# One attention and routing kernel: a unit's x and the last blocks of q and k are transposed at another place

## The chip, the core and the metric

The kernel runs on one core of one Trainium2 chip. The metric is the device time of one launch in microseconds (us). Before the change the median of three runs is 667.53 us (664.54 to 668.78).

## The reference

Two blocks follow each other. The first is attention over a sliding window of 64 keys, for 8 batches, 8 heads, 576 positions and heads of width 64:

```
scores = scale * np.matmul(q, k.transpose(0, 1, 3, 2))
mask = (rel >= 0) & (rel < window)
scores = np.where(mask, scores, -1000000000.0)
attn = softmax(scores)
x = np.matmul(attn, v)        # then (B, H, S, D) -> (B*S, H*D) = 4608 x 512
```

The second sends each of the 4608 rows of x to the one of eight experts that has the largest logit, and scales the result with the gate:

```
expert_idx = np.argmax(x @ w_gate, axis=1)
h = np.maximum(x_sorted[lo:hi] @ w1[e], 0.0)      # 512 -> 1024
y_sorted[lo:hi] = h @ w2[e]                        # 1024 -> 512
out = gate_w[:, None] * y
```

## The kernel before

The attention fills the first 180 us or so of the span. It is cut into 16 units (two batches and two heads each), and a unit into three steps of three blocks of 128 positions; eight blocks are full ones, and the ninth holds the last 64 positions of both batches. So there are 48 steps `s`, and the function `step(s)` writes out by hand what each engine gets, in the order in which it gets it. Each engine works its list off in that order, and nothing is moved by a scheduler.

In `step(s)`, TensorE gets: the scores of step s+1 (`scored`, L762), the product of the weights of step s-1 with v (`weighted`, L822), the transposes of the softmax weights of step s (`flipped`, L796, "flips"), and the transposes of q and k for step s+3 (`turned`, L726). Flips and `turned` transpose 64 rows at a time: the upper 64 partitions go into one bank of PSUM, the lower 64 into another, matmul by matmul in turn. VectorE (DVE) gets the mask and the row maxima of step s+1 (`masked`, six pairs of rows at L775), the division of step s-1 (`divided`, L832, L833, L836), and the copy of the first bank of flips (L805). ScalarE (ACT) gets six exponentials (`softened`, L785), the copy of the second bank of flips (L805) and both copies of `turned` (L732).

Three kinds of step take turns:

- s % 3 == 0: as told.
- s % 3 == 1 (for 13 of the 16 units; called a unit step below): `unit_turned` also transposes the finished x of the unit before, eight blocks in 16 transposes of 64 rows (L864), into two banks. It is called between the scores and `weighted`. VectorE's copy of its first bank (L871) is queued at once, so ahead of `divided`; ScalarE's copy of the second (called at L1178) after the copies of the flips. The ninth block's x rides along in the flips' banks (L800).
- s % 3 == 2 (called an end step below): the logits of a unit (`logits`, L908, and VectorE's L913 or L915) come ahead of the flips, and `turned` handles the ninth block of q and k of the next unit: two transposes of 128 rows (L717) into a bank of its own, and one copy by ScalarE (L720).

All transposes (flips, `turned`, `unit_turned`) and the logits take their banks from one ring of five, `tr_ring` (banks 2, 3, 4, 5 and 7, which the lists of instructions call bank_83, bank_84, bank_85, bank_86 and bank_88), always the next one. Who takes a bank waits until the copy out of it, five takings ago, is through. The scores have two banks of their own (bank_81, bank_82), the product with v has bank_87.

GpSimd (POOL) sorts q and k into the order that `turned` reads (L671) and shifts v (L698 to L706); SyncE issues the loads. The routing of every fourth unit puts further VectorE rows (L940 to L1007) into the steps that follow it. After the attention TensorE goes through the experts in tiles of 256 rows.

Of the kernel before, what the change touches and what calls it, by code (L numbers as in the profile page):

```python
# [36 lines left out]
def kernel(  # L37
# [10 lines left out]
    nc = tc.nc  # L48
    P = nc.NUM_PARTITIONS
    B, H, S, D = q.shape  # L50
# [8 lines left out]
    NV = NB // 2  # L59
    SM = NV * P  # L60
    BG = 2
# [29 lines left out]
    ident = consts.tile([P, P], F32, name="ident")  # L91
# [40 lines left out]
    banks = [Memory(banks_p.tile([P, 512], F32, name=f"bank{i}")) for i in range(8)]  # L132
# [54 lines left out]
    with tc.tile_pool(name="tmp", bufs=1) as tmp:  # L187
# [8 lines left out]
        for i in range(BG):  # L196
# [14 lines left out]
            out=behind[:], in_=behind[:], pattern=[[-1, P]], compare_op=ALU.is_ge, fill=0.0, base=0,  # L211
# [45 lines left out]
    NST = NTB // ST  # L257
# [346 lines left out]
    with tc.manual_schedule(), ExitStack() as brief, ExitStack() as held:  # L604
# [7 lines left out]
        sc_ring, tr_ring = cycle((0, 1)), cycle((2, 3, 4, 5, 7))  # L612
# [7 lines left out]
            out=half[:, n : n + 1], in_=half[:, n : n + 1], fill=MASKED, pattern=[[0, 1], [rest[0], P]],  # L620
# [16 lines left out]
        units = [(bg, g) for bg in range(B // BG) for g in range(NG)]  # L637
        NU = len(units)

        halves = (slice(0, D), slice(D, P))  # L640
        qks, sides, rests, Ts, xss, xTs, lgs, logits_of = {}, {}, {}, {}, {}, {}, {}, {}
        NMAIN = BG * NV
# [3 lines left out]
        whole_x = lambda s: s % NST == 1 and 0 <= (s - NST) // NST < NWHOLE  # L646
# [61 lines left out]
        def turned(s, which=(0, 1)):  # L708

            u, c = divmod(s, NST)  # L710
            bg, g = units[u]
            if c == 0:
                Ts[u] = qkT_m(u % 2 * 2 * NTB * P, 2, NTB, P)
            if c == BG:
                tr = banks[next(tr_ring)](0, NV, P)
                for n, t in enumerate(rests[bg][0:2]):
                    nc.tensor.transpose(  # L717
                        out=tr[:, n, :], in_=t[:, 2 * g : 2 * g + 2].rearrange("p h d -> p (h d)"), identity=ident[:]
                    )
                nc.scalar.copy(out=Ts[u][:, :, BG * NV, :], in_=tr[:, 0:2, :])  # L720
                return
            trs = [banks[next(tr_ring)](0, len(which), D, NV) for _ in range(2)]
            for i, n in enumerate(which):
                for j in range(NV):
                    for tr, r in zip(trs, halves):
                        nc.tensor.transpose(  # L726
                            out=tr[:, i, :, j], in_=sides[s][n][r, j].rearrange("p h d -> p (h d)"),
                            identity=ident[r, r],
                        )
            to = Ts[u][:, which[0] : which[-1] + 1, c * NV : (c + 1) * NV, :].rearrange("d n t s -> d n (t s)")  # L730
            for a, tr in enumerate(trs):
                (nc.vector.tensor_copy if (s, a) == (0, 1) or (s, which) == (1, (0,)) else nc.scalar.copy)(  # L732
                    out=to[:, :, a * NV * D : (a + 1) * NV * D], in_=tr.rearrange("d n p j -> d n (p j)")
                )
# [46 lines left out]
        def softened(prs, mx, which):  # L781
            for n in which:
                h, m = divmod(n, ST)
                y = prs[h][:, m, :]
                nc.scalar.activation(out=y, in_=y, func=AF.Exp, scale=-1.0, bias=mx[:, h, m : m + 1])  # L785

        def flipped(s, prs):
            pTs = []
            n = 2 * ST * D
            last_x = n + D if whole_x(s) else n  # L790
            trs = [banks[next(tr_ring)](0, last_x) for _ in range(2)]
            for h in range(2):
                for m in range(ST):
                    at = (h * ST + m) * D
                    for tr, r in zip(trs, halves):
                        nc.tensor.transpose(out=tr[:, at : at + D], in_=prs[h][r, m, :], identity=ident[r, r])  # L796
            if last_x > n:
                bg, g = units[s // NST - 1]
                for tr, r in zip(trs, halves):
                    nc.tensor.transpose(  # L800
                        out=tr[:, n:last_x], in_=xss[bg, NST - 1][r, ST - 1, g * P : (g + 1) * P], identity=ident[r, r]
                    )
            for a, tr in enumerate(trs):
                pT = att.tile([P, n + D], F32, name=f"pT{a}")
                (nc.scalar.copy if a or s in (N - 5, N - 4) else nc.vector.tensor_copy)(  # L805
                    out=pT[:, 0:last_x], in_=tr
                )
                pTs.append(pT[:, 0:n].rearrange("p (h m s) -> p h m s", h=2, m=ST))
                if last_x > n:
                    x_rests.setdefault(s // NST - 1, []).append(pT[:, n:last_x])  # L810
            return pTs
# [45 lines left out]
        def unit_turned(u):  # L857

            bg, g = units[u]
            xTs[u] = xp.tile([P, NTB, P], F32, name="xT")  # L860
            trs = [banks[next(tr_ring)](0, NMAIN, D) for _ in range(2)]
            for t in range(NMAIN):
                for tr, r in zip(trs, halves):
                    nc.tensor.transpose(  # L864
                        out=tr[:, t, :], in_=xss[bg, t // ST][r, t % ST, g * P : (g + 1) * P], identity=ident[r, r]
                    )
            copies = [
                partial(copy, out=xTs[u][:, 0:NMAIN, r], in_=tr)
                for tr, r, copy in zip(trs, halves, (nc.vector.tensor_copy, nc.scalar.copy))
            ]  # L870
            copies[0]()  # L871
            return copies[1]

        def x_of(u, t):

# [238 lines left out]
        N = NU * NST  # L1114
# [30 lines left out]
        n = 0  # L1145
# [10 lines left out]
        def step(s):  # L1156
            n_exp = 2 * ST
            if 0 <= s + 1 < N:
                prs[s + 1], mx = masked(s + 1, scored(s + 1))
                softened(prs[s + 1], mx, range(2 if s == N - 2 else n_exp))  # L1160
            if whole_x(s):
                second_half = unit_turned(s // NST - 1)
            if 0 <= s - 1 < N:
                px = weighted(s - 1, pTs.pop(s - 1))
            for op in between.pop(s, ()):
# [1 line left out]
            if s == N - 2:  # L1167
                pTs[s] = flipped(s, prs.pop(s))
                softened(prs[s + 1], mx, range(2, n_exp))
# [3 lines left out]
            if 0 <= s < N and s != N - 2:  # L1173
                pTs[s] = flipped(s, prs.pop(s))
                if s == N - 1:
                    form_all(turn((1,)))
            if whole_x(s):
                second_half()  # L1178
            if 0 <= s - 1 < N:
                bg, g = units[(s - 1) // NST]  # L1180
                if g == NG - 1 and s + 1 < N:
# [2 lines left out]
            if s >= 0 and s % NST == 0:  # L1184
                u = s // NST
# [9 lines left out]
            if s == -2:  # L1195
                turned(1, (1,))
            elif s + 3 < N:
                if s == -1:
                    turned(1, (0,))
                turned(s + 3)  # L1200
# [6 lines left out]
            if ripe:  # L1207
                bg = (s - 3) // (NG * NST)
# [8 lines left out]
        for s in range(-3, N):  # L1217
            if s == N - 1:
                tr_ring = cycle((4, 5, 7, 1))
            step(s)  # L1220
# [5 lines left out]
        tr_ring = cycle((4, 5))  # L1226
# [180 lines left out]
```

## Time and profile before

| | |
|---|---|
| median of three runs | 667.53 us |
| the profiled execution's own time | 668.92 us |
| its span | 667.2 us |
| granted TensorE clock, mean | 0.997 of full speed |
| TensorE busy / VectorE / ScalarE / GpSimd | 97% / 73% / 41% / 54% of the span |

The shares are means over stages with different limits: ScalarE is busy some 90% of the time in the attention and about 20% behind it. Starts and durations of rows are in us from the span's start. A row's duration overlaps with that of the next row of its engine, so that what a row costs its engine is read from start to start. A count such as "x24" on a row of scores counts two matmul instructions for one product in float32; a transpose is one.

### The profile page before, as it was taken

How to read it: one execution, taken by the hardware profiler on the slowest of the kernel's cores; microseconds unless marked ns; L12 is line 12 of the kernel's file. 1: busy time of each engine (PE TensorE's matmuls, PEld its weight loads, DVE VectorE, ACT ScalarE, POOL GpSimd, SP SyncE). 2: the span in 40 equal slices, each digit the busy share in tenths (PEclk: the TensorE clock that was granted, in tenths of full speed). 3: DMA queues.
4: the chain of work that ended last, by engine and by line, in shares of the span. 5: the costliest groups of instructions: out<-in, count | busy, mean ns of one | idle time of the engine just before them, and what ended most of it. 6: DMA issues, size and time to landing. Idle time of an engine off the chain costs nothing. (4 is left out here: it accounts for less than half of the span.)

```text
span 667.2 us, 19140 instructions
## 1 busy us (share of the span) xinstructions
PE 645.8 (97%) x7436; PEld 566.7 (85%) x7437; DVE 488.0 (73%) x1587; ACT 276.4 (41%) x669; POOL 360.4 (54%) x425
## 2 busy tenths in 40 slices
PE   8999999999899999999999999999999999999996
PEld 5878888877789897979999999899699799699995
DVE  6988999989758766757667667567775686576864
ACT  6988999988722222122212212112331222222220
POOL 8458577496723177376730735645385666373112
PEclk9999999999999999999999999999999999999998
DMA  9799989896420823617210460460264171212012
GB/s 239 177 226 315 235 251 255 252 269 197 140 85 2 312 69 121 235 53 253 83 51 17 132 234 18 126 242 17 67 208 153 54 269 49 66 43 65 12 56 65
DMA packets 91686, 95.27 MB, mean 143 GB/s; under 512 B 54063, under 2 KB 70463, under 8 KB 91552
## 3 DMA queue, kind: packets, MB, share of 16 engines
q1 hardware_dynamic: 71104, 36.68, 20.5%
q0 software_dynamic: 8640, 26.88, 12.6%
q10 hardware_dynamic: 11808, 29.95, 12.4%
q8 instruction: 81, 1.33, 0.8%
q14 instruction: 53, 0.43, 0.2%
HBM read 74.32 MB, written 20.74 MB: 142 GB/s over the span
## 5 line engine op out<-in xcount | busy, mean ns | idle before, releaser
L340 DVE STREAM_TRANSPOSE v_m<-xg 32x256 f32<-32x256 f32 x304 | 132.3, 435 | 17.5 <-ACT xg L325 11.6
L296 POOL DMA_INDIRECT xg<-x_dram,at_g x42 | 44.4, 1056 | 163.2 <-ACT qk_m L352 121.3
L369 PE MATMUL bank<-qk_m,s 128*128 128x128 f32 x1024 | 122.6, 275 | 0.0
L369 PEld LDWEIGHTS bank<-qk_m,s 128*128 128x128 f32 x1024 | 118.3, 192 | 0.4 <-issue 0.2
L785 ACT ACTIVATE pr<-pr,mx 128x128 f32<-128x128 f32 x288 | 89.8, 394 | 14.6 <-DVE mx L775 14.4
L369 PE MATMUL bank<-qk_m,w 128*128 128x128 f32 x768 | 94.1, 276 | 1.3 <-DVEq L1308 0.9
L369 PEld LDWEIGHTS bank<-qk_m,w 128*128 128x128 f32 x768 | 90.3, 192 | 4.8 <-issue 4.4
L775 DVE CUSTOM_DVE_ANT_0 pr<-bank,mask 128x128 f32<-128x128 f32 x288 | 64.7, 286 | 13.7 <-PE bank L762 12.8
L315 POOL DMA_INDIRECT out_dram<-v_m,at_s x42 | 42.6, 1013 | 57.4 <-DVE v_m L411 53.3
L411 DVE TENSOR_TENSOR v_m<-bank,v_m 128x256 f32<-128x256 f32 (+1 forms) x95 | 43.8, 480 | 40.0 <-PE bank L415 26.4
L149 POOL TENSOR_TENSOR s<-w 128x1024 f32<-128x1024 f32 x22 | 52.2, 2372 | 0.0
L415 PE MATMUL bank<-qkT_m,v_m 128*128 128x256 f32 x216 | 48.1, 379 | 0.0
L822 PE MATMUL bank<-v_m,pT 128*64 128x65 f32 x1152 | 46.9, 227 | 0.5 <-DVE pT L805 0.5
L822 PEld LDWEIGHTS bank<-v_m,pT 128*64 128x64 f32 x1152 | 40.1, 137 | 7.8 <-DVE pT L805 3.7
L376 ACT COPY qk_m<-bank 128x512 f32<-128x512 f32 x16 | 9.4, 586 | 88.9 <-PE bank L369 65.6
L415 PEld LDWEIGHTS bank<-qkT_m,v_m 128*128 128x128 f32 x216 | 41.0, 190 | 5.6
L352 ACT COPY qk_m<-v_m 128x512 f32<-128x512 f32 x38 | 21.6, 615 | 57.2 <-DVE v_m L340 57.2
L762 PE MATMUL bank<-qkT_m 64*64 64x128 f32 x1152 | 43.6, 278 | 0.8 <-issue 0.5
L671 POOL COPY side<-qk_m 128x512 f32<-128x512 f32 x61 | 35.7, 611 | 8.4 <-DMA qk_m<-in_q_dram 3.9
L381 DVE TENSOR_TENSOR qk_m<-bank,qk_m 128x512 f32<-128x512 f32 x16 | 11.1, 692 | 38.2 <-PE bank L369 25.0
L415 PE MATMUL bank<-s,v_m 128*128 128x256 f32 x168 | 37.4, 379 | 0.0
L762 PEld LDWEIGHTS bank<-qkT_m 64*64 64x64 f32 x1152 | 31.3, 132 | 6.7 <-issue 1.6
(230 smaller groups left out, 1214.1 us busy)
## 6 DMA issues: line engine op xcount, KB each, us to landing
w<-in_moe_w_dram ACTq DMA_DIRECT2D x11, 2048.0 KB, 7.8
qk_m<-in_q_dram SPq DMA_DIRECT2D x32, 256.0 KB, 5.1
v_m<-in_v_dram SPq DMA_DIRECT2D x64, 128.0 KB, 5.4
qk_m<-in_k_dram SPq DMA_DIRECT2D x30, 256.0 KB, 5.6
qk_m<-in_moe_w_dram ACTq DMA_DIRECT2D x3, 2048.0 KB, 10.5
x_dram<-xs POOLq DMA_DIRECT2D x4, 512.0 KB, 6.3
w<-in_moe_w_dram SPq DMA_DIRECT2D x4, 512.0 KB, 5.6
x_dram<-xs SPq DMA_DIRECT2D x4, 512.0 KB, 4.4
```

Of the source, the lines that this page charges most:

```text
L149: op()
L296: G.indirect_dma_start(out=xg_all[:, c], out_offset=None, in_=x_dram[:, :], in_offset=bass.IndirectOffsetOnAxis(ap=at_g[:, c : c + 1], axi ...
L315: put = G.indirect_dma_start(out=out[:, :], out_offset=bass.IndirectOffsetOnAxis(ap=at_s[:, c : c + 1], axis=0), in_=ys[c], in_offset=None ...
L340: V.transpose(out=xn[b * QD : (b + 1) * QD, :, :, a * QD : (a + 1) * QD], in_=rows[a * QD : (a + 1) * QD, :, :, b, :],)
L369: nc.tensor.matmul(acc[:, f, :], lhsT=a[:, g, f * P : (f + 1) * P], rhs=b[:, g, :], start=(first and f == 0 and g == 0), stop=(g == HG - 1 ...
L411: plus = lambda out, a, b: V.tensor_tensor(out=out, in0=a, in1=b, op=ALU.add)
L415: nc.tensor.matmul(acc, lhsT=a[:, f, :], rhs=b[:, f, :], start=(start and f == 0), stop=(stop and f == HF - 1), skip_group_check=True,)
L671: copy(out=side[:], in_=t[:, c].rearrange("p h j d -> p j h d"))
L762: nc.tensor.matmul(out_, lhsT=qT[rows, t, a * WINDOW : (a + 1) * WINDOW], rhs=rhs, start=True, stop=True, skip_group_check=True,)
L775: V.tensor_tensor_reduce(out=prs[h][:, m, :], in0=scs[h][:, m, :], in1=mask[:, m0 + m, :], scale=-scale, scalar=-2 * MASKED, op0=ALU.add, ...
L785: nc.scalar.activation(out=y, in_=y, func=AF.Exp, scale=-1.0, bias=mx[:, h, m : m + 1])
L822: nc.tensor.matmul(px[a * D : (a + 1) * D, h, m, :], lhsT=pTs[a][:, h, m, :], rhs=vt[:, h, :], start=True, stop=True, skip_group_check=True,)
```

## The change

The transposes of a unit's x move from between scores and `weighted` to behind the flips, ahead of `turned`, and both copies of them are queued there. The ninth block of q and k of units 1 to 15 is transposed in `flipped` of the end step, 64 rows at a time, into columns 384 to 511 of the flips' two banks; VectorE copies one half of it and ScalarE the other. Unit 0 keeps the old way.

```
@@ turned @@
             if c == BG:
+                if u:
+                    return
@@ flipped @@
-            trs = [banks[next(tr_ring)](0, last_x) for _ in range(2)]
+            ends = s // NST + 1 if s % NST == BG and s // NST + 1 < NU else None
+            trs = [banks[next(tr_ring)](0, 512) for _ in range(2)]
...
+            if ends is not None:
+                bg, g = units[ends]
+                for i, t in enumerate(rests[bg][0:2]):
+                    at = n + i * D
+                    for tr, r in zip(trs, halves):
+                        nc.tensor.transpose(
+                            out=tr[:, at : at + D], in_=t[r, 2 * g : 2 * g + 2].rearrange("p h d -> p (h d)"),
+                            identity=ident[r, r],
+                        )
             for a, tr in enumerate(trs):
                 pT = att.tile([P, n + D], F32, name=f"pT{a}")
-                (nc.scalar.copy if a or s in (N - 5, N - 4) else nc.vector.tensor_copy)(
-                    out=pT[:, 0:last_x], in_=tr
-                )
+                copy = nc.scalar.copy if a or s in (N - 5, N - 4) else nc.vector.tensor_copy
+                copy(out=pT[:, 0:last_x], in_=tr[:, 0:last_x])
+                if ends is not None:
+                    copy(
+                        out=Ts[ends][:, :, BG * NV, halves[a]],
+                        in_=tr[:, n : n + 2 * D].rearrange("d (n s) -> d n s", n=2),
+                    )
@@ unit_turned @@
-            copies = [
-                partial(copy, out=xTs[u][:, 0:NMAIN, r], in_=tr)
-                for tr, r, copy in zip(trs, halves, (nc.vector.tensor_copy, nc.scalar.copy))
-            ]
-            copies[0]()
-            return copies[1]
+            for tr, r, copy in zip(trs, halves, (nc.vector.tensor_copy, nc.scalar.copy)):
+                copy(out=xTs[u][:, 0:NMAIN, r], in_=tr)
@@ step @@
-            if whole_x(s):
-                second_half = unit_turned(s // NST - 1)
             if 0 <= s - 1 < N:
                 px = weighted(s - 1, pTs.pop(s - 1))
...
             if whole_x(s):
-                second_half()
+                unit_turned(s // NST - 1)
```

TensorE's list in the first unit step (s = 4), before. The names are the bank written and what is read; of each group of transposes the first two stand, one for each of its two banks:

```order
L762 MATMUL bank_82<-qkT_m 64x128
L864 MATMUL bank_85<-ident,xs 128x64
L864 MATMUL bank_86<-ident,xs 128x64
...
L822 MATMUL bank_87<-v_m,pT_623 64x65 x2
L796 MATMUL bank_88<-ident,pr_577 128x64
L796 MATMUL bank_83<-ident,pr_577 128x64
...
L800 MATMUL bank_88<-ident,xs 128x64
L800 MATMUL bank_83<-ident,xs 128x64
L726 MATMUL bank_84<-ident,side_555 128x64
L726 MATMUL bank_85<-ident,side_555 128x64
```

The same place with the change (L764, L838, L799, L803, L880 and L728 are what L762, L822, L796, L800, L864 and L726 were):

```order
L764 MATMUL bank_82<-qkT_m 64x128
...
L799 MATMUL bank_84<-ident,pr_580 128x64
L799 MATMUL bank_85<-ident,pr_580 128x64
...
L803 MATMUL bank_84<-ident,xs 128x64
L803 MATMUL bank_85<-ident,xs 128x64
L880 MATMUL bank_86<-ident,xs 128x64
L880 MATMUL bank_88<-ident,xs 128x64
...
L728 MATMUL bank_83<-ident,side_558 128x64
L728 MATMUL bank_84<-ident,side_558 128x64
```

The second bank of `turned` was the first bank of `unit_turned` (bank_85), and is now the first bank of the flips of the same step (bank_84). It is so in all 13 unit steps, since six banks are taken in each from a ring of five.

VectorE's list in the same step, before: the last row of `masked`, the copy of x, `divided`, the copy of the flips, the first row of the next `masked`:

```order
L775 ISA pr_670,mx<-bank_82,mask 128x128
L775 ISA mx 128x1
L871 COPY xT<-bank_85 128x8x64
L832 TENSOR_SCALAR rec<-bank_87 128x6
L833 RECIPROCAL rec<-rec 128x6
L836 TENSOR_TENSOR xs<-bank_87,rec 128x2x3x64
L805 COPY pT_732<-bank_88 128x448
L775 ISA pr_777,mx<-bank_81,mask 128x128
```

With the change (L777, L848, L849, L852, L818 and L884 are what L775, L832, L833, L836, L805 and L871 were):

```order
L777 ISA pr_673,mx<-bank_82,mask 128x128
L777 ISA mx 128x1
L848 TENSOR_SCALAR rec<-bank_87 128x6
L849 RECIPROCAL rec<-rec 128x6
L852 TENSOR_TENSOR xs<-bank_87,rec 128x2x3x64
L818 COPY pT_717<-bank_84 128x448
L884 COPY xT<-bank_86 128x8x64
L777 ISA pr_780,mx<-bank_81,mask 128x128
```

The copy of x went from the front of `divided` to behind the copy of the flips.

VectorE's list around an end step (s = 5) with the change; before, L820 is not there:

```order
L852 TENSOR_TENSOR xs<-bank_87,rec 128x2x3x64
L925 COPY lgT<-bank_85 96x128
L818 COPY pT_839<-bank_86 128x384
L820 COPY qkT_m<-bank_86 128x2x64
L777 ISA pr_861,mx<-bank_81,mask 128x128
```

One copy of 128 columns is added there to VectorE's list. ScalarE's list has the same copy for the other half in place of its copy of 256 columns (L720).

## Rows read from the trace of the kernel before

**Rows 1.** The page, busy time, share of the span, instructions:

```profile
PE 645.8 (97%) x7436; PEld 566.7 (85%) x7437; DVE 488.0 (73%) x1587; ACT 276.4 (41%) x669; POOL 360.4 (54%) x425
```

**Rows 2.** Stretch 20 to 150: us, PE, PEld, DVE, ACT, POOL busy, clock, DMA, GB/s

```profile
20.00:150.00 130.00, 125.09 (x3129) 106.95 (x3127) 117.54 (x653) 117.21 (x341) 85.42 (x162) 1.00 0.90 248
```

**Rows 3.** Timeline, TensorE, one unit step: start, duration, row, idle before

```profile
43.63 0.89 PE L762 MATMUL bank<-qkT_m 64*64 64x128 f32 x24
44.45 0.86 PE L864 MATMUL bank<-ident,xs 64*128 64x64 f32 x16
45.25 0.97 PE L822 MATMUL bank<-v_m,pT 128*64 128x65 f32 x24
46.15 0.59 PE L796 MATMUL bank<-ident,pr 64*128 64x64 f32 x12
46.57 0.23 PE L800 MATMUL bank<-ident,xs 64*128 64x64 f32 x2
46.63 0.76 PE L726 MATMUL bank<-ident,side 64*128 64x64 f32 x16
47.33 0.44 PE L762 MATMUL bank<-qkT_m 64*64 64x128 f32 x6
```

**Rows 4.** Timeline, VectorE, the same unit step

```profile
45.95 0.69 DVE L871 COPY xT<-bank 128x512 f32<-128x512 f32 x1
46.55 0.16 DVE L832 TENSOR_SCALAR rec<-bank 128x6 f32<-128x6 f32 x1
...
47.44 0.62 DVE L805 COPY pT<-bank 128x448 f32<-128x448 f32 x1
48.26 0.29 DVE L775 CUSTOM_DVE_ANT_0 pr<-bank,mask 128x128 f32<-128x128 f32 x1 [0.21 <-PE bank L762]
```

**Rows 5.** Timeline, TensorE, a unit step with routing behind it

```profile
88.82 0.71 PE L726 MATMUL bank<-ident,side 64*128 64x64 f32 x15 [0.68 <-DVE xT L871]
89.46 0.89 PE L762 MATMUL bank<-qkT_m 64*64 64x128 f32 x24
```

**Rows 6.** Timeline, VectorE, the same step

```profile
88.08 0.68 DVE L871 COPY xT<-bank 128x512 f32<-128x512 f32 x1
...
90.10 0.55 DVE L1007 TENSOR_TENSOR lo<-low,lane 128x384 bf16<-128x384 bf16 x1
90.56 0.28 DVE L775 CUSTOM_DVE_ANT_0 pr<-bank,mask 128x128 f32<-128x128 f32 x1
```

**Rows 7.** One line (L871): its rows, then who waited for it (us, times)

```profile
L871 DVE COPY xT<-bank x13: 680/686/689, 24.4 to 152.2; 128x512 f32<-128x512 f32 x13
...
  PE bank L726: 3.4, 5
```

**Rows 8.** Timeline, TensorE, the unit step that waits for GpSimd

```profile
36.56 1.02 PE L726 MATMUL bank<-ident,side 64*128 64x64 f32 x16 [1.26 <-POOL side L671]
```

**Rows 9.** Timeline, TensorE, an end step from its flips on

```profile
49.83 0.59 PE L796 MATMUL bank<-ident,pr 64*128 64x64 f32 x12
50.35 0.44 PE L717 MATMUL bank<-ident,qk_m 128*128 128x128 f32 x2
50.72 0.34 PE L762 MATMUL bank<-qkT_m 64*64 64x128 f32 x4
```

**Rows 10.** Timeline, VectorE, that end step, then one with routing in it

```profile
50.43 0.28 DVE L915 TENSOR_TENSOR lgT<-bank,lgT 96x128 f32<-96x128 f32 x1
50.63 0.54 DVE L805 COPY pT<-bank 128x384 f32<-128x384 f32 x1
51.66 0.29 DVE L775 CUSTOM_DVE_ANT_0 pr<-bank,mask 128x128 f32<-128x128 f32 x1 [0.48 <-PE bank L762]
...
83.13 0.29 DVE L775 CUSTOM_DVE_ANT_0 pr<-bank,mask 128x128 f32<-128x128 f32 x1 [0.27 <-PE bank L762]
```

**Rows 11.** Groups by line and shape, 20 to 150 us: copies of nearby sizes

```profile
L913 DVE COPY lgT<-bank 96x128 f32<-96x128 f32 x3 | 0.8, 280 | 0.1
...
L720 ACT COPY qkT_m<-bank 128x256 f32<-128x256 f32 x13 | 4.9, 378 | 0.0
```

## Prediction

> **What bounds the kernel now.** I read the page first: TensorE is busy for 97% of the span [rows 1]. The change touches only the attention, so the next view is busy time by stretch, for 20 to 150 us [rows 2]: of 130 us TensorE has 125, VectorE 118, ScalarE 117, at full clock. Three engines are near their limit there, so busy time does not say which sets the pace. The timelines of TensorE and VectorE, laid side by side step by step, do.
>
> Take the unit step at 43.63 [rows 3, 4]. TensorE starts the scores, then x, `weighted`, flips, and at 46.63 `turned`; the next scores start at 47.33. VectorE's copy of x runs from 45.95 to 46.64, and 0.69 us after its end the next scores start. At 88 us the same pair stands 0.70 apart: copy done at 88.76, scores at 89.46 [rows 5, 6]. I looked up this distance in all 13 unit steps. It is 0.69 or 0.70 in eleven and 0.72 in a twelfth; the thirteenth, near 36 us, is held by GpSimd. The reason stands in TensorE's list: the second transpose of `turned` needs the bank out of which the copy of x reads; once it is free, 0.06 us later, the 15 transposes that are left take 0.63 us. Where TensorE arrives early, the wait is seen as such: 3.4 us in five of 13 steps [rows 7]. So in a unit step **the release of one bank by VectorE sets when the next scores start**. In an end step TensorE never waits; it runs its list at its own pace, and VectorE waits for the scores (0.48 us at 51.66) [rows 10].
>
> **Unit step, what is added: a later release.** With the change the second bank of `turned` is the first bank of the flips, so TensorE waits for VectorE's copy of the flips. VectorE gets to it behind `masked` and `divided`, with the copy of x now behind it. From rows 4, counted from the end of `masked` (45.95): before, the release was at 0.69. Now `divided` starts 0.60 earlier than at 46.55, so the copy of the flips starts at 47.44 - 45.95 - 0.60 = 0.89 and ends 0.62 later, at 1.51. The release comes **1.51 - 0.69 = 0.82 us later**.
>
> Does TensorE arrive later than that anyway? In its new order it has scores 0.82, `weighted` 0.90, flips and L800 0.48, x at 16 x 0.035 = 0.56 (the 12 flips take 0.42 [rows 3]), together 2.8 us after the start of the scores. The release comes at 45.95 - 43.63 + 1.51 + 0.06 = 3.9. So TensorE waits about 1.0 us in each such step, and whatever the x transposes save by their new neighbours (0.80 before [rows 3] against 0.56) vanishes in that wait. A delay of `weighted` by ScalarE's copy of the flips would vanish there too. VectorE's own work is the same in sum; what stood behind its copy of x now stands behind its copy of the flips.
>
> Of the 0.82 us, what reaches the next `masked` depends on whether VectorE was late there. In five steps it was not (at 48.26 it had even been idle for 0.21 us [rows 4]): all 0.82 counts. In seven, routing rows made VectorE late. At 90.56 it starts 1.10 after the scores instead of 0.94 [rows 5, 6], so 0.16 is absorbed; over the seven it is 0.15 to 0.28, mean 0.19, leaving 0.63. The thirteenth is the step where TensorE waits 1.26 us for GpSimd's sorted q and k [rows 8]. GpSimd had waited for a load of v issued long before, so this point stays where it is and swallows the shift of the first unit. Counted are 4 x 0.82 + 7 x 0.63 = **+7.7 us**.
>
> **End step, what is removed and added.** TensorE: from the first flip to the next scores 0.89 us (49.83 to 50.72), of which 0.37 are the two transposes L717 and 0.10 is the distance that flips followed by L717 have more (0.52) than flips followed by L800 (0.42) [rows 3, 9]. New: 12 flips 0.42, four more transposes of the same form 0.14, and some 0.03 to the scores, 0.60 in all. **-0.29 us per end step.** Bounds for the four: 0.14 by the flips, which have their very form, and 4 x 0.18 by L717, at which nothing would be saved. I take the first.
>
> VectorE gets a copy of 128 columns from PSUM. The trace has none with this output; nearest are L913 (280 ns) and L775 (290 ns). From start to start, L915 of the same size costs 0.20 (50.43 to 50.63) [rows 10, 11]. I take 0.20; bounds are nothing, where VectorE has that much idle time, and 0.29. It lies ahead of `masked`, so the gain is the smaller of 0.29 and the idle time there less 0.20 (the later scores of the unit step also take away VectorE's lateness, up to 0.28, ahead of this). Behind the GpSimd point there are 12 end steps of units with logits. In eight the idle time suffices, as at 51.66; the other four, as at 83.13 with 0.27 idle, give 0.07 to 0.24, 0.56 together. One more, at the end of the attention, where VectorE never waits, loses 0.2. Sum: 8 x 0.29 + 0.56 - 0.2 = **-2.7 us**. ScalarE exchanges a copy of 256 columns (378 ns [rows 11]) for one of 128, and what it saves goes into its waiting. The later end of the flips' bank (0.14) is covered: VectorE's copy of it starts 0.37 after the last flip (50.63 against 50.26).
>
> **Sum.** +7.7 - 2.7 = **+5.0 us**, all in the attention; behind it nothing changes, and it begins when the attention ends. The span would be 672.2 and this execution, 1.7 us longer than its span, 673.9. It lies 1.4 us above the median of the runs, so for the median I add to that: 667.5 + 5.0 = **672.5 us**, 0.75% slower.
>
> **Rivals.** (a) **TensorE's order alone decides**, because the bank is free in time or VectorE gets ahead. Then a unit step would lose the extra time of L864, up to 0.24 us, but no more than VectorE's idle time, 0.2 in three steps and nothing in the others: -0.6. With -2.7 from the end steps that is 664.2. For it speaks that the change lets transposes of one form (64 rows by 128 columns) follow each other, and rows 9 show 0.10 us where the form changes. Against it: the bank in TensorE's new list, and eleven distances of 0.69 or 0.70. [...] Chance 0.10.
>
> (b) **VectorE becomes the bound of the end steps.** If the new copy costs 0.29 and VectorE is late at most scores, because routing and later releases pile up, the end steps give nothing or lose 0.2 each: +7.7 to +10.7, so 675 to 678. The point from which it decides is an idle time of less than 0.2 us ahead of `masked` in most end steps. For it: VectorE is busy 118 of 130 us. Against it: 0.48 us in plain units, and the new wait in the unit step gives VectorE fresh idle time. Chance 0.15.
>
> (c) **The wait is there but half absorbed**, because routing rows of VectorE fill the time while TensorE waits, more than the 0.19 that I count: +3.5 instead of +7.7, so 668.3. For it: seven unit steps have such rows. Against it: they lie behind the copy of the flips, as before. Chance 0.12.
>
> **How the numbers follow.** My forecast has 0.63, with a range of its own of 670 to 675 (0.03 us in the size of the wait over 11 steps is 0.3 us; the price of the copy between nothing and 0.29 is 2 us either way; 1.5 us is the spread of the runs). Holding out one tenth on either side over all cases gives 667 to 677. About 1%, 6.7 us, is what a measurement of this kernel can tell from no change. Slower by more than that (over 674.2) are most of (b) and the upper end of my forecast: 0.26. Faster by more would be below 660.9, which none of the cases reaches: 0.03. The rest is 0.71.
>
> **What would show it.** In the changed profile: a wait of TensorE at `turned` (now L728) for VectorE's copy of the flips (L818), about 1 us in each of some 12 unit steps, 10 to 12 us in all, and none for the copy of x (L884); unit steps of 4.5 us in place of 3.7; end steps of 3.1 in place of 3.4 in units without routing; VectorE's new copy (L820) 15 times at 0.2 to 0.3 us. I would be wrong if that wait is under 0.5 us, if `masked` in the end steps no longer waits for scores at all, or if the time behind the attention changes by more than 2 us.

## The result, and the profile after

The changed kernel takes **675.51 us** (median of 6 runs, 674.27 to 677.14) against 667.51 us (664.54 to 670.01) for the kernel before beside it: ratio **1.0121, interval 1.0101 to 1.0141**. That is +8.0 us. Forecast were 672.5 us (667 to 677), same 0.71 and slower 0.26: the time lies in the range, but the change is slower by more than 1%, which had the smaller chance. The profiled execution took 676.05 us with a span of 674.2 (before 668.92 and 667.2).

The page's busy line answers rows 1; the stretch from 20 to 150 us (us, then busy time of PE, PEld, DVE, ACT, POOL, then the granted clock, DMA share, GB/s) answers rows 2:

```profile
PE 644.1 (96%) x7466; PEld 566.2 (84%) x7467; DVE 491.5 (73%) x1601; ACT 277.9 (41%) x670; POOL 361.8 (54%) x425
```

```profile
20.00:150.00 130.00, 115.79 (x2983) 100.55 (x2985) 115.00 (x633) 112.62 (x325) 83.92 (x159) 0.97 0.89 245
```

TensorE now stands idle 14 of these 130 us, where it was 5, and its mean clock there is 0.97 instead of 1.00. The waits from 0 to 215 us (engine, what it waited for, us in total, times, longest) say for whom:

```profile
PE bank L728 <- DVE pT L818: 14.1, 13, 1.8
DVE pr L777 <- PE bank L764: 14.0, 19, 1.4
```

The first is the wait of the forecast, at the bank, by the engine and for the copy that it named. One plain unit step, on TensorE and then on VectorE (rows 3 and 4 show the same step before):

```profile
42.75 0.89 PE L764 MATMUL bank<-qkT_m 64*64 64x128 f32 x24
...
45.10 0.66 PE L880 MATMUL bank<-ident,xs 64*128 64x64 f32 x16
45.60 0.22 PE L728 MATMUL bank<-ident,side 64*128 64x64 f32 x1
46.55 0.71 PE L728 MATMUL bank<-ident,side 64*128 64x64 f32 x15 [0.72 <-DVE pT L818]
47.19 0.89 PE L764 MATMUL bank<-qkT_m 64*64 64x128 f32 x24
```

```profile
45.88 0.61 DVE L818 COPY pT<-bank 128x448 f32<-128x448 f32 x1
46.41 0.68 DVE L884 COPY xT<-bank 128x512 f32<-128x512 f32 x1
48.13 0.29 DVE L777 CUSTOM_DVE_ANT_0 pr<-bank,mask 128x128 f32<-128x128 f32 x1 [1.04 <-PE bank L764]
```

One transpose of `turned` goes through, the second waits until the copy of the flips ends at 46.49, and the scores follow 0.70 us later. The step takes 4.44 us (42.75 to 47.19) instead of 3.70. VectorE then waits 1.04 us for scores. The copy of x, which was waited for in rows 7, is waited for no more.

The end step behind it (TensorE from the flips on, then the new copies by engine: count, shortest/median/longest ns, first and last start):

```profile
49.70 0.59 PE L799 MATMUL bank<-ident,pr 64*128 64x64 f32 x12
50.12 0.29 PE L811 MATMUL bank<-ident,qk_m 64*128 64x64 f32 x4
50.34 0.89 PE L764 MATMUL bank<-qkT_m 64*64 64x128 f32 x24
```

```profile
L820 ACT COPY qkT_m<-bank x16: 258/271/273, 20.1 to 176.7; 128x128 f32<-128x128 f32 x16
L820 DVE COPY qkT_m<-bank x14: 277/278/281, 20.0 to 165.9; 128x128 f32<-128x128 f32 x14
```

From the first flip to the scores it is 0.64 us, where rows 9 had 0.89; the end step takes 3.15 us instead of 3.39. VectorE makes the new copy 14 times, not 15: in the last end step ScalarE copies both halves.

Three end steps, though, take 4.60, 4.63 and 4.61 us. Here is the one at 90.78, TensorE and then windows of 1 us:

```profile
90.15 0.71 PE L728 MATMUL bank<-ident,side 64*128 64x64 f32 x15 [1.72 <-DVE pT L818]
90.78 0.97 PE L764 MATMUL bank<-qkT_m 64*64 64x128 f32 x24
91.68 1.62 PE L838 MATMUL bank<-v_m,pT 128*64 128x65 f32 x24
93.23 1.28 PE L920 MATMUL bank<-xT,wg 128*32 128x128 f32 x14
...
95.38 0.89 PE L764 MATMUL bank<-qkT_m 64*64 64x128 f32 x24
```

```profile
91.00:92.00 1.00, 1.00 (x30) 0.75 (x24) 0.37 (x4) 0.91 (x2) 0.27 (x1) 0.73 0.61 103
92.00:93.00 1.00, 1.00 (x24) 1.00 (x20) 1.00 (x11) 0.82 (x3) 0.00 (x0) 0.50 1.09 301
93.00:94.00 1.00, 1.00 (x18) 0.81 (x17) 0.73 (x5) 1.00 (x4) 0.00 (x0) 0.50 1.04 386
```

TensorE waits for nothing there: it runs at a granted clock of 0.50 (called half clock below) for some 3.4 us. The three stretches cost 4.60 + 4.63 + 4.61 - 3 x 3.15 = 4.4 us. They followed unit steps in which `turned` had waited 1.72, 1.59 and 1.61 us. The attention before has no such stretch: its granted clock is 1.00 in every window of 0.5 us from 20 to 180 us.

**The account**, step by step from scores to scores up to the last block's scores (172.08 us before, 179.81 after): twelve unit steps +9.6 us, the unit step that GpSimd held at 36 us (rows 8) -1.2, since its wait is gone, the 13 end steps -0.7 (without the slow clock -5.1), all others 0.0. That is +7.7. Behind the attention the changed kernel is 0.7 us shorter, so the spans differ by 7.0.

Two of these terms are not the change's own. The wait for GpSimd stands in the profile of before and in none of the others, as told below. And of the 5.1 us, 2.0 are four end steps of the profile of before that took 3.48 to 4.31 us instead of 3.39, two of them with gaps of 0.34 and 0.65 us in which TensorE waits for nothing that the profile shows. The shorter end steps themselves give the other 3.1 us.

### The profile page after: what moved, and what is told of

It is laid out like the page before. It is cut to its first block, busy times and chain, and to the rows that moved or that the text cites. A ratio compares the mean times of both kernels' runs of the same rounds, so it can differ in the third digit from the quotient of the medians.

```text
span 674.2 us, 19230 instructions
## 1 busy us (share of the span) xinstructions
PE 644.1 (96%) x7466; PEld 566.2 (84%) x7467; DVE 491.5 (73%) x1601; ACT 277.9 (41%) x670; POOL 361.8 (54%) x425
## 5 line engine op out<-in xcount | busy, mean ns | idle before, releaser
L787 ACT ACTIVATE pr<-pr,mx 128x128 f32<-128x128 f32 x288 | 89.7, 391 | 14.1 <-DVE mx L777 13.8
L777 DVE CUSTOM_DVE_ANT_0 pr<-bank,mask 128x128 f32<-128x128 f32 x288 | 64.7, 286 | 15.0 <-PE bank L764 14.0
L149 POOL TENSOR_TENSOR s<-w 128x1024 f32<-128x1024 f32 x22 | 52.2, 2375 | 0.0
L838 PEld LDWEIGHTS bank<-v_m,pT 128*64 128x64 f32 x1152 | 42.0, 142 | 11.7 <-DVE pT L818 8.1
L838 PE MATMUL bank<-v_m,pT 128*64 128x65 f32 x1152 | 48.9, 233 | 2.1 <-DVE pT L818 1.3
L764 PE MATMUL bank<-qkT_m 64*64 64x128 f32 x1152 | 44.2, 281 | 0.8 <-issue 0.5
L728 PE MATMUL bank<-ident,side 64*128 64x64 f32 x512 | 25.4, 226 | 14.4 <-DVE pT L818 14.1
```

Of the source, the lines that this page charges most:

```text
L149: op()
L764: nc.tensor.matmul(out_, lhsT=qT[rows, t, a * WINDOW : (a + 1) * WINDOW], rhs=rhs, start=True, stop=True, skip_group_check=True,)
L777: V.tensor_tensor_reduce(out=prs[h][:, m, :], in0=scs[h][:, m, :], in1=mask[:, m0 + m, :], scale=-scale, scalar=-2 * MASKED, op0=ALU.add, ...
L838: nc.tensor.matmul(px[a * D : (a + 1) * D, h, m, :], lhsT=pTs[a][:, h, m, :], rhs=vt[:, h, :], start=True, stop=True, skip_group_check=True,)
```

## The experiments

All times of a kernel stand beside those of the kernel before on the same chip. "Stops" are times in which TensorE waits for nothing that the profile shows ("issue"); their sums are over 20 to 170 us. A profile shows one execution; those of the first four kernels below were 2.1 to 6.5 us slower than the median of their kernel, so sums read from them need not hold for the others.

### Each half alone

Only the end steps (the change with its unit steps put back):

```
-            for tr, r, copy in zip(trs, halves, (nc.vector.tensor_copy, nc.scalar.copy)):
-                copy(out=xTs[u][:, 0:NMAIN, r], in_=tr)
+            copies = [
+                partial(copy, out=xTs[u][:, 0:NMAIN, r], in_=tr)
+                for tr, r, copy in zip(trs, halves, (nc.vector.tensor_copy, nc.scalar.copy))
+            ]
+            copies[0]()
+            return copies[1]
...
+            if whole_x(s):
+                second_half = unit_turned(s // NST - 1)
...
-                unit_turned(s // NST - 1)
+                second_half()
```

> The ninth blocks of q and k in the flips' banks, the transposes of x back at their old place. Theory A (the loss sits in the unit steps: a later release of the bank, and stretches at half clock that follow its long waits): end steps 0.25 us shorter, no wait of TensorE for the copy of the flips ahead of turned, no stretch at half clock, 664 to 665.5 us. Rival B (the loss sits in the end steps: three of them took 4.6 us in the changed kernel because four transposes now wait for loads and VectorE has a copy more): those long end steps stay, 668 to 670 us.

669.25 us (665.67 to 673.66) against 667.82: ratio 1.0019, 0.9991 to 1.0046. The end steps do fall to 3.15 us and a plain unit of three steps from 9.82 to 9.50, but the time does not. The rival's number came nearer, though not by its mechanism. In this profile three things stand against the gain. Where routing rows fill VectorE's list, the copy makes it late (its idle time ahead of the scores behind an end step fell from 0.49 to 0.04 in plain units, and in routing units it has next to none); the 13 steps behind the end steps took 0.9 us more in all than before. The last block's scores start 0.3 us sooner than before (171.77 against 172.08), but what follows them takes 2.8 us more. And TensorE has more stops, 3.9 us where the profile of before has 1.5:

```profile
94.66 0.65 PE L764 MATMUL bank<-qkT_m 64*64 64x128 f32 x11 [0.77 <-issue]
100.91 0.28 PE L838 MATMUL bank<-v_m,pT 128*64 128x65 f32 x2 [1.30 <-issue]
```

Only the unit steps (the change with its end steps put back):

```
-                if u:
-                    return
...
-            ends = s // NST + 1 if s % NST == BG and s // NST + 1 < NU else None
+            ends = None
```

> The transposes of x behind the flips, the ninth blocks of q and k at their old place (128 rows, own bank, ScalarE). Theory A: unit steps of 4.44 us where no routing is in them, a wait of TensorE for VectorE's copy of the flips in all 13, 1.3 us or more in some, half-clock stretches behind some of these; +7.7 us and 1.5 us for each half-clock stretch, 676 to 679 us. Rival B: unit steps cost less, the end steps carried the loss: 670 to 672 us.

678.38 us (675.37 to 682.35), ratio 1.0138, 1.0115 to 1.0161, as the forecast's mechanism has it. Plain unit steps take 4.51 us, 0.82 more than before and so the forecast's own number, with the wait in its place:

```profile
47.68 0.71 PE L726 MATMUL bank<-ident,side 64*128 64x64 f32 x15 [0.79 <-DVE pT L816]
```

Half clock came three times in this attention: behind the two longest of these waits (1.73 and 1.62 us), and behind a stop of 1.70 us. So the loss belongs to the unit steps.

### The same order on TensorE, another on VectorE

The change with VectorE's copy of the flips ahead of `divided` in unit steps:

```
+            if whole_x(s):
+                pTs[s] = flipped(s, prs.pop(s))
...
-            if 0 <= s < N and s != N - 2:
+            if 0 <= s < N and s != N - 2 and not whole_x(s):
```

> The changed kernel, but in unit steps VectorE copies the flips ahead of the division, so that the bank is free 0.62 + 0.06 us after the last masked row in place of 1.57. Theory A: the next scores start 3.6 us after the last ones (4.44 in the changed kernel, 3.7 before), no wait over 1 us beyond what routing causes, no half-clock stretch, the end steps keep their gain: 663 to 665.5 us. Rival B (the bank's release is not what counts, TensorE's new order or the end steps cost the time): 672 us or more.

670.35 us (668.46 to 676.31), ratio 1.0026, 0.9997 to 1.0056: with TensorE's order and banks left as in the change, most of the loss is gone, and the granted clock is 1.00 in every window of 1 us from 15 to 170 us. VectorE, then TensorE, in a plain unit step:

```profile
44.27 0.62 DVE L818 COPY pT<-bank 128x448 f32<-128x448 f32 x1 [0.31 <-PE bank L803]
```

```profile
44.95 0.27 PE L728 MATMUL bank<-ident,side 64*128 64x64 f32 x2 [0.22 <-DVE pT L818]
```

TensorE's wait is 0.22 instead of 0.72, and the step 3.95 us. I had expected 3.6: the copy now waits itself, for the flips. The expected 663 to 665.5 us were missed by 5 us. Nearly as much more stands in stops: 6.0 us (the longest 1.47 and 1.34), where the profile of before has 1.5; that they make up the whole miss was not shown.

The counter-test leaves TensorE's order and banks as before the change and queues both copies of x behind those of the flips:

```
-            copies[0]()
-            return copies[1]
+            return lambda: form(copies)
```

> The kernel before with one edit: in a unit step VectorE and ScalarE copy the turned x behind the copies of the flips, not in front of `divided`. TensorE's order and banks are those of before, so `turned` still waits for the copy of x. Theory A (the release of that bank by VectorE sets the next scores, one for one): the release comes at 0.89 + 0.62 + 0.60 = 2.11 us after `masked` instead of 0.69, 1.42 later, that is 1.7 times the change's 0.82. Unit steps of about 5.1 us in place of 3.7, TensorE waiting about 1.5 us for the copy of x in some 12 of them, and without any slower clock 667.5 + 12 x 1.3 = 683 us (680 to 686). With the clock: the changed kernel ran at half clock for 3.4 us behind three of its four longest waits (1.59, 1.61, 1.72), at 1.45 us each; if waits of this length do it here too, four to twelve such stretches come on top, 688 to 700. Rival (the step's length comes from TensorE's new order and banks, not from when VectorE releases): this order is the old one, so unit steps stay within 0.3 us of 3.7 and the time within 4 us of before.

695.15 us (692.71 to 697.75) against 669.92: ratio 1.0387, 1.034 to 1.0434. The later release, without any new order on TensorE, costs 25 us with all that follows from it. The wait, and a plain unit step followed by an end step at full clock, then the unit step at 80 us and its end step at half clock (both copies of x now have the line L149, that of a helper which queues them):

```profile
PE bank L726 <- DVE xT L149: 21.8, 13, 2.1
```

```profile
61.55 0.71 PE L726 MATMUL bank<-ident,side 64*128 64x64 f32 x15 [1.57 <-DVE xT L149]
62.19 0.89 PE L762 MATMUL bank<-qkT_m 64*64 64x128 f32 x24
...
63.90 0.74 PE L907 MATMUL bank<-xT,wg 128*32 128x128 f32 x14
...
84.99 0.71 PE L726 MATMUL bank<-ident,side 64*128 64x64 f32 x15 [1.56 <-DVE xT L149]
85.63 0.89 PE L762 MATMUL bank<-qkT_m 64*64 64x128 f32 x24
...
87.80 1.28 PE L907 MATMUL bank<-xT,wg 128*32 128x128 f32 x14
```

Plain unit steps take 5.43 us, 1.74 more than before; I had said 1.42. The rest is `divided`, which in the same step starts 0.32 us behind the end of `masked` (59.06), since the copy of x no longer stands ahead of it and it has to wait for `weighted`:

```profile
59.38 0.17 DVE L832 TENSOR_SCALAR rec<-bank 128x6 f32<-128x6 f32 x1 [0.23 <-PE bank L822]
```

1.42 and 0.32 make the 1.74. Six end steps take 4.8 to 5.2 us at the lower clock, 8.7 us in all. Without them the profiled execution, 692.88 us, would have 684.2, inside the 680 to 686 of the theory; so both parts of it hold, release and clock.

### The wait kept, but filled

The change with four products of 512 columns of constants in front of `turned` in unit steps, into a bank that `turned` overwrites:

```
+            for _ in range(busy):
+                nc.tensor.matmul(
+                    trs[0].rearrange("d n p j -> d (n p j)"), lhsT=ones[:],
+                    rhs=mask[:, 0:4].rearrange("p a b -> p (a b)"), start=True, stop=True, skip_group_check=True,
+                )
...
-                turned(s + 3)
+                turned(s + 3, busy=4 if whole_x(s) else 0)
```

> The changed kernel with four matmuls of 512 columns in bfloat16 in front of turned in each unit step, into the bank that turned overwrites next: 0.9 us of TensorE work for nothing, which fits into the wait of about 1 us. Theory A (the half-clock stretches come from TensorE standing idle in this wait): granted clock 1.00 throughout, no end step of 4.6 us, unit steps unchanged at 4.44, 671 to 673.5 us. Rival C (the half-clock stretches have another cause, or the four matmuls lengthen the step): 675 us or more.

677.09 us (674.82 to 683.63), ratio 1.0123, 1.01 to 1.0145: nothing won. Plain unit steps:

```profile
45.93 1.04 PE L726 MATMUL bank<-mask,ones 128*128 128x512 bf16 x4
46.89 0.71 PE L733 MATMUL bank<-ident,side 64*128 64x64 f32 x16
47.54 0.89 PE L769 MATMUL bank<-qkT_m 64*64 64x128 f32 x24
```

They keep their 4.44 to 4.57 us, and behind none of the 13 is the clock low: every end step that follows takes 3.14 to 3.16 us, but for one at 4.43 with a stop of 1.00 in it, one at 3.43 and the last at 3.81, as in the change. So the clock part of the expectation holds for the waits, the longest of which is 1.00 us here; full clock throughout, as expected, it was not. The time part does not hold: the stops are 4.6 us here, 0.5 in the change, and with the longest the clock itself falls to 0.50, for 6.8 us from 67.5 on:

```profile
68.07 0.69 PE L733 MATMUL bank<-ident,side 64*128 64x64 f32 x8 [2.56 <-issue]
```

### Are the stops a matter of loads?

Loads of v run while the stops come: the stops in the profile of before end at 64.90, 70.60 and 144.56 us (0.53, 0.34 and 0.65 us), and SyncE issues loads of v from 59.28 to 64.13, 67.80 to 72.12 and 140.61 to 145.09 us, which land 6.2 us later (median, from 60 to 72 us). So I suspected them. That the stops are late instructions (theory D below) rests on two queues that the page of before names "instruction", with 81 packets, 1.33 MB, and 53 packets, 0.43 MB; which stop they belong to it does not say. Four kernels leave the loads of v out from the fourth unit on (NVR is 3): that of before, the change, the end steps alone, and the change with the wait filled; their routing then differs, and what follows the attention is another, much longer program, so their times are compared with each other alone.

```
+            if u >= NVR:
+                return
```

> The kernel before with the loads of v left out from the fourth unit on (those units read the v of an earlier unit, so x, the routing and the number of tiles differ from the real ones; it is compared with the other kernels that leave out the same). Theory D (TensorE's unexplained stops of 0.3 to 2.5 us in the attention, put down to issue, are pages of its instructions that come late behind the loads): these stops vanish or sum to under 0.5 us between 20 and 170 us (1.5 us in the kernel before), and no wait for GpSimd's v. Rival (the stops have nothing to do with the loads): 1 us or more of them stay.

> The changed kernel with the same loads of v left out. Theory A and D: the attention is longer than with the kernel before and the same loads left out by the waits alone, 12 or 13 unit steps of 4.44 us or more and end steps of 3.15, +4 to +6 us, and 1.5 us more for each stretch at half clock, of which there are 0 to 3; in all +4 to +10 us. If the unexplained stops carried the loss, the two lie within 3 us of each other.

> Ends only (the transposes of x at their old place) with the same loads of v left out. Theory A and D: without the unexplained stops the gain of the end steps is seen, -2 to -3 us against the kernel before with the same loads left out. Rival E (VectorE's new copy takes the gain back wherever routing rows stand in the steps): 0 to -1 us, with VectorE late by more than before at the scores of the steps behind an end step.

> The changed kernel with four matmuls of 512 columns in the wait of each unit step, and the same loads of v left out. Theory A (the half-clock stretches come from TensorE standing idle in the long waits): no half-clock stretch behind a unit step, so 0 to 4 us less than the changed kernel with the same loads left out, by 1.5 us for each such stretch that that one shows. Rival C (other cause of the half clock): as many such stretches as without the four matmuls, and no gain.

Medians: before 1653.13 us, the change 1662.09, end steps alone 1654.44, filled 1662.07. The change loses 9.0 us here too, the end steps alone gain nothing, and filling gains nothing. The stops stay: 1.6 us before, 3.2, 4.9 and 3.6 in the others. So these loads of v are not their cause; the loads of q, k and the weights ran on. In the attention of the change half clock came once, behind a wait of 2.12 us (2.11 and 1.70 had none behind them), with the wait filled never. The longest stop of the change:

```profile
55.16 0.67 PE L766 MATMUL bank<-qkT_m 64*64 64x128 f32 x16 [1.21 <-issue]
```

### Does VectorE's new copy eat the gain of the end steps?

The end steps alone (the unit steps put back as above), with both halves copied by ScalarE, and both by VectorE:

```
-                    copy(
+                    nc.scalar.copy(          # in the other kernel: nc.vector.tensor_copy(
                         out=Ts[ends][:, :, BG * NV, halves[a]],
                         in_=tr[:, n : n + 2 * D].rearrange("d (n s) -> d n s", n=2),
                     )
...
```

> The kernel before with the ends of q and k turned in the flips' banks (the change's end steps alone), but both halves copied out by ScalarE, so that VectorE's list is that of before. Theory F (the gain of the end steps, 0.24 us of TensorE each, is lost because VectorE's added copy of 0.28 us makes it late at the next `masked`): the lateness that the end steps alone brought to the c = 0 steps goes, and the time falls by 12 x 0.24 = 2.9 us against the kernel before, less what ScalarE's two copies of 128 columns cost beside one of 256 (it has slack in end steps): 665 us, 664 to 666.5. Rival G (the gain is lost whatever VectorE does, because an earlier TensorE runs into longer stops for which the profile names nothing, or into loads and GpSimd's work at their own points): the time is that of the end steps alone, 668 to 670, with end steps of 3.15 us all the same.

> As the run with both halves copied by ScalarE, but both by VectorE, one copy of 0.28 us more than the change puts there, so the suspected cost is doubled. Theory F (VectorE's copy eats the end steps' gain): VectorE has now 0.4 to 0.56 us more in each end step, more than the 0.48 us of idle time before the next `masked` in plain units, so every end step is paced by VectorE: 13 x 0.1 to 0.25 = 1.5 to 3 us on top of the end steps alone, 670 to 672.5. Rival G (VectorE's copy is not what counts): within 1 us of the run with both by ScalarE.

By ScalarE 672.31 us (671.55 to 675.54), ratio 1.005, 1.0027 to 1.0073; by VectorE 670.31 us (668.7 to 673.11), ratio 1.0007, 0.9986 to 1.0028. Theory F, as the main cause, falls: with VectorE's copy doubled the time is no worse than with one (1.0019). Rival G, which put both runs within 1 us of each other, missed too: by ScalarE it takes 2.0 us more. That run shows a wait that I had not seen coming; ScalarE, then TensorE:

```profile
30.31 0.27 ACT L820 COPY qkT_m<-bank 128x128 f32<-128x128 f32 x1 [0.62 <-DVE pT L818]
30.47 0.48 ACT L818 COPY pT<-bank 128x384 f32<-128x384 f32 x1
```

```profile
31.01 0.91 PE L838 MATMUL bank<-v_m,pT 128*64 128x65 f32 x20 [0.16 <-ACT pT L818]
```

ScalarE's first small copy reads the bank that VectorE is still copying, waits 0.62 us for it, and holds its own copy of the flips up; in plain units the step behind an end step takes 3.28 instead of 2.73 us. That outweighs the end steps' gain. So this run says nothing of VectorE's copy alone. By VectorE, both small copies take 0.41 us from start to start of their neighbours, and VectorE has no idle time left ahead of the next scores:

```profile
49.39 0.49 DVE L820 COPY qkT_m<-bank 128x128 f32<-128x128 f32 x2
49.80 0.28 DVE L777 CUSTOM_DVE_ANT_0 pr<-bank,mask 128x128 f32<-128x128 f32 x1
```

Still the step lasts 2.73 us and a plain unit 9.56: TensorE is not held up. At its last scores but one this kernel is 2.1 us ahead of the profile of before. Then a step of 5.48 us (before 3.93), with a wait of 1.27 us for GpSimd (before 0.39) and half clock in it, takes 1.6 of it back, and what follows takes 1.5 us more than before.

## Why the prediction was right, and where it was not

**The release sets the unit step: right.** Forecast 0.82 us per plain unit step, measured 0.75, and 0.82 where the unit steps alone were changed; forecast a wait of 10 to 12 us in all, about 1.0 each, measured 14.1 in 13 steps, 0.72 in plain ones (0.95 from the first transpose of `turned` on, 45.60 to 46.55). Counted from `masked`, as the forecast did, the release is later by its number: in ten of the twelve steps, the one held by GpSimd left out, the loss is 0.81 to 0.83 us plus the change in how long after the scores `masked` starts (in plain ones 0.96 us instead of 1.04). The transposes of x became shorter as said (0.50 us from 45.10 to 45.60, where it was 0.80), and that vanished in the wait. Moving VectorE's copy alone brought most of it back in one kernel and made three times the loss in another.

**"0.16 is absorbed; ... leaving 0.63" failed.** In the seven steps with VectorE late I took 0.19 us off for it. Six of them lost 0.65 to 1.13 us and the last 0.21; the seven make 5.7 us in place of 4.4. The lateness had cost nothing before: the end step at 89.46 [rows 5, 6], with `masked` 0.16 late, lasted 3.39 us like the plain ones, so there was nothing to save. What did move the loss was VectorE's lateness at the other end of the step. Behind the end step with the new copy it had no idle time, so that in the unit step at 85.29 `masked` starts 2.04 us after the scores, and 1.90 before (in the step at 84.92); that step lost 0.96. In the last unit step `masked` came sooner, 1.79 us after the scores instead of 2.58. The first `masked` row of the step at 84.92 before, then of that at 85.29:

```profile
86.82 0.28 DVE L775 CUSTOM_DVE_ANT_0 pr<-bank,mask 128x128 f32<-128x128 f32 x1
```

```profile
87.33 0.28 DVE L777 CUSTOM_DVE_ANT_0 pr<-bank,mask 128x128 f32<-128x128 f32 x1
```

The eleven steps that I counted make +8.8 us, not +7.7; with the first unit's, +9.6.

**The point held by GpSimd was not fixed.** I let it swallow the first unit's shift. The first unit's +0.75 stayed, and the 1.26 us of rows 8 disappeared. Net: -0.4 instead of 0. But this wait is missing in all eleven other profiles too, among them those of the kernel before with fewer loads of v and with nothing but the copies of x moved. GpSimd's row behind a load of v, in the profile of before and in the latter:

```profile
32.76 0.62 POOL L698 COPY v_m<-v_m 64x520 f32<-64x520 f32 x1 [4.09 <-DMA v_m<-in_v_dram]
```

```profile
30.70 0.62 POOL L698 COPY v_m<-v_m 64x520 f32<-64x520 f32 x1 [3.39 <-DMA v_m<-in_v_dram]
```

So the wait looks like one of that execution and not of the kernel; why the load landed late in it was not tested.

**The end step: right in its own length, wrong in the sum.** -0.24 us was measured for -0.29 forecast, and VectorE's copy costs the 0.20 us that I took: in plain units its idle time ahead of the next scores shrank from 0.48 to 0.04 us, by 0.24 for the earlier scores and by 0.20 for the copy (0.28 us long). In the changed kernel the 13 end steps gave 3.1 us before the clock is counted, for 2.7 forecast; the other 2.0 of the 5.1 us are long steps of the profile of before. Alone, however, they gave no time that can be measured, in three forms and in the run with fewer loads. Where that went is not settled: the stops are longer in those profiles (3.9 against 1.5 us in one, 4.9 against 1.6 in another, but 1.4 and 1.7 with the copies on one engine), half-clock stretches stand at their attention's end (at 178, 178 and 170 us) that the profile of before does not have, and in the three forms what follows the last block's scores takes 1.5 to 2.8 us more than before.

**The clock was missing.** The forecast read "at full clock" from rows 2 and kept it. Behind three of the waits that it predicted the clock fell to 0.50: 4.4 us in the profiled execution, a term that the sum does not have. It varies from run to run: three of six ran at a mean clock of 0.994 to 0.995 and took 674.3 to 675.0 us, three at 0.991 to 0.993 and took 676.1 to 677.1. With the wait filled, none of the 26 unit steps of two kernels had half clock behind it; with the wait doubled, six of 13 had. The price is read from the longer end steps: no run won the time back, and the filled ones show more stops.

**That the sum came so near is in part luck.** Between the spans it is +7.0 us for +5.0. The unit steps (+1.1) and the clock (+4.4) were too low in the forecast; the GpSimd point (-0.4), the end steps with the long ones of before (-2.4) and the time behind the attention (-0.7) took most of that back.

**Rivals.** TensorE's order alone (664.2) is excluded by the wait. VectorE as the bound of the end steps gave the right time range (675 to 678), which holds the result where the range of the forecast's own case (670 to 675) just misses it, but by the wrong road: at full clock all end steps but the last take 3.15 us, in routing units too, though VectorE has 0.1 us or less of idle time ahead of the scores behind them. The half-absorbed wait is excluded by the 5.7 us of the seven steps; only in the last of them did most of it vanish.

## What to carry to other kernels

Where banks come from a ring, count the takings per step: six takings from a ring of five make the last wait for the first of the same step, and here the place of that copy in VectorE's list then set TensorE's pace (14.1 us of waits in 13 steps). The wait put on TensorE cost twice here, as a wait (9.6 us in twelve steps) and by what the clock did behind it (4.4 us), so price both; and lateness of an engine is worth something only if the step with it was longer than the step without (3.39 us both here).

## What the runs showed of the hardware

**Behind waits of 1.5 to 2.1 us TensorE's clock often fell, though not each time.** At `turned`, 12 of 22 such waits in four kernels were followed by half clock (0.50), and no shorter one was. In the changed kernel 1.59, 1.61 and 1.72 us were, 1.81 was not. With the copy of x last, the first five unit steps waited 1.56 or 1.57 us and kept full clock; of the eight behind them six lost it, after 1.56 to 2.09 us, and waits of 1.97 and 1.65 did not. Elsewhere half clock came behind stops of 1.70 and 1.55 us, with one of 2.56 us, once behind a wait of 1.27 us for GpSimd, and three times behind the attention's last scores (at 178, 178 and 190 us). So the length of the wait alone does not decide. A stretch of half clock behind a unit step cost some 1.4 to 1.5 us: end steps of 4.60 to 4.63 us in place of 3.15 in the changed kernel, 8.7 us over six with the copy of x last.

**TensorE stops for which no releaser shows** take 0 to 6 us of the attention, from kernel to kernel, in single gaps of up to 2.56 us. The kernel whose TensorE waited longest at `turned` (21.8 us) had none between 20 and 170 us, the one with its copy ahead of `divided` the most (6.0 us). That instructions come late in them was the author's theory, and no run showed it; leaving out loads of v did not remove them (1.6 us before, 3.2, 4.9 and 3.6 in the others), and their cause stays open.

**Two engines at one bank.** With both halves copied by ScalarE, its copy out of a bank of PSUM that VectorE was still copying began only behind VectorE's copy, after 0.62 us in the row above and 9.7 us in 14 copies from 0 to 215 us; what makes it wait was not tested.
